# Attention and a squared-ReLU channel mix on one core: the left-over keys of two pairs multiplied in four quadrants, the token mix through PSUM

## The chip, the cores and the metric

The kernel runs on one core of a Trainium2 chip. The metric is the device time of one execution in microseconds (us). Engines: TensorE (PE; PEld are its weight loads), VectorE (DVE), ScalarE (ACT), GpSimd (POOL), and SyncE (SP), which here only issues transfers.

## The reference

Soft-capped attention over 8 batches, 12 heads, 448 tokens, 64 channels a head, then a channel mix in which each token is blended with the one before it:

```python
scores = cap * np.tanh(scale * q @ k.T / cap)
attn = np.exp(scores - max);  attn = attn / (attn.sum(-1) + 1e-9)
x = (attn @ v) as (B, S, 768)
xk = mu_k * x + (1 - mu_k) * x_prev          # x_prev: x one token earlier
xr = mu_r * x + (1 - mu_r) * x_prev
k = np.maximum(xk @ w_k, 0)                  # 768 -> 1024
out = sigmoid(xr @ w_r) * (k * k @ w_v)      # w_v: 1024 -> 768
```

All inputs are float32, `w_k`, `w_v`, `w_r` are float64.

## The kernel before

**Stages.** A first loop of 55 steps does the attention of 48 pairs of heads (six a batch), the rounding of the float64 weights, and, from step 7 on, the key product `xk @ w_k`. Its result and `x` go to DRAM. A second stage of 28 chunks of 128 tokens computes `xr @ w_r`, `k * k @ w_v` and the output; the change does not touch it.

**The order of a step.** Nothing is scheduled by a tool: each engine runs its instructions in the order in which the string `STEP` names the operations. Step i works on several pairs at once: scores (`S0` to `S3`), `tanh`, `exp`, `red` on pair i; `V` (values), `gather`, `recip`, `rec_store`, `rec_load` on pair i - 1; `norm`, `mix_old`, `mix_new`, `x_high`, `x_low`, `x_store` on pair i - 2; `qk_high`, `qk_low` on i + 2 and `load_qk` on i + 3. `K` (four in a step) is a quarter of the step's key product, 6 matmuls; `f` is one of the five VectorE operations that round a weight tile; up to step 9, five steps load a second weight tile.

**Scores.** A pair has two heads, h = 0 and 1. Queries and keys lie with head 0 on partitions 0 to 63 and head 1 on 64 to 127, so scores of both heads run as two matmuls of 64 rows each. The 448 keys are cut into three groups g of 128 and 64 left over. Each product is made of three (high by high, low by high, high by low). The left-over keys of both heads make one group, g = 3: head 0's 64 scores on the first half of the partitions, head 1's on the second. `tanh` and `exp` on ScalarE turn the scores (`s` in PSUM, two buffers) into `p`.

**Values.** `values` multiplies the exponentials by v, in float32: for each group two matmuls, one a head, each with 64 columns of the stationary tile `rv` and so half of the array's columns; `pv[p, 0:S]` gets head h on its half of the partitions. In group 3 the stationary tile of a head has v on that head's half of the rows, and zeros on the other, since the moving rows hold the exponentials of both heads:

```python
nc.tensor.matmul(pv[p, 0:S], v[:, g, h, :], ph[:, h if g < 3 else 0, :], start=(g == 0), stop=(g == 3))
```

`pv` has two buffers (`ps_v`), each a PSUM bank.

**Sums.** `red` on VectorE sums the exponentials over keys into `r1`, by a transposing reduction (one for each of g = 0 to 2, two halves for g = 3). A step later `gather` brings four parts of `r1` together by four transfers (`sq`), `recip` sums them, inverts and transposes (three VectorE instructions), `rec_store` writes the 2 x 448 results to DRAM (`rec_d`), and `rec_load` reads them back, spread over 64 partitions a head (`r`). One more step later `norm` writes `X = pv * r`.

**The mix.** `mix_old` (ScalarE) writes `xk = (1 - mu_k) * X` one token back, `mix_new` (VectorE) adds `mu_k * X` to it, `x_high` and `x_low` (GpSimd) split the sum into a high and a low half for the key product.

**The key product.** `kpart` issues the matmuls of `K`. A feature chunk of 128 takes 18 of them; its sum `kps` has two PSUM buffers, emptied by `relu` on ScalarE, which stands at three places of a step. The order in `key_order` delays the last of six pairs of a batch, so that two chunks end together in a batch's second step (step 6b + 2), and the next `K` then needs a buffer that the relu behind `exp2` frees.

**Queues.** All transfers but `k_store` are issued on SP, in the order of `STEP`; an issue that waits holds up those behind it. `load_qk` stands behind `rec_load`, which waits until `rec_store` has landed.

Of the kernel before, what the change touches and what calls it, by code (L numbers as in the profile page):

```python
# [9 lines left out]
F32 = mybir.dt.float32  # L10
F32R = mybir.dt.float32r
AF = mybir.ActivationFunctionType
ALU = mybir.AluOpType
# [3 lines left out]
B, H, S, D = 8, 12, 448, 64  # L17
# [8 lines left out]
P = 128  # L26
# [9 lines left out]
KM = 3 * P  # L36
KC = KM + P
LAG = 7
HALF = (slice(0, 64), slice(64, 128))
NB = 2 * S // 32  # L40
# [3 lines left out]

STEP = """gather load_v weight_load more weight_low S0 S1 V S2 f f f f f weight_rest tanh0 exp0 red0 norm
weight_sum tanh1 recip rec_store exp1 red1 mix_old mix_new K qk_high qk_low x_high x_low tanh2 relu k_store
K exp2 red2 relu k_store S3 K K tanh3 exp3 red3 relu k_store weight_abs rec_load load_qk x_store weight_store"""


def f(ap):
# [3 lines left out]
class Body:  # L56
# [61 lines left out]
    def init_sums(self, pool):  # L118


        nc = self.nc
        self.r1, self.sq, self.sr = [], [], []
        for j in range(2):
            self.r1.append(pool.tile([P, NB, 4], F32, name=f"r1_{j}"))
            nc.gpsimd.memset(self.r1[j], 0.0)
            for h in range(2):
                p = slice(64 - 64 * h, 96 - 64 * h)
                nc.vector.tensor_copy(self.r1[j][p, h * NB // 2:(h + 1) * NB // 2, 3], self.grd[p].to_broadcast([32, NB // 2]))
            self.sq.append(pool.tile([32, 4, NB, 4], F32, name=f"sq_{j}"))
            self.sr.append(pool.tile([32, 32], F32, name=f"sr_{j}"))  # L130
            nc.gpsimd.memset(self.sr[j], 1.0)

    def init_attn(self):
        self.raw, self.QK, self.rawv, self.S, self.P32, self.PV, self.R, self.rs = ({} for _ in range(8))

# [4 lines left out]
            self.nc.sync.dma_start(t[:, c], self.qk[i // NP, i % NP][:, c])  # L142

    def load_v(self, i):
        t = self.rawv[i] = self.rawp.tile([P, 4, 2, D], F32, name="rv")
        self.nc.sync.dma_start(t.rearrange("p c h d -> p (c h d)"), self.v[i // NP, i % NP])

    def qk_high(self, i, e="p"):
# [10 lines left out]
    def row_maxima(self, i):  # L159

        nc, qk = self.nc, self.QK[i]
        m = self.up.tile([S // 4, 8], F32, name="m", bufs=1)
        for h in range(2):
            t = HALF[h]
            for c in range(4):
                if c % 2 == 0:
                    s = self.ps_s.tile([P, 2, 512], F32, name="s")
                o = s[0:S // 4, c % 2, 0:S]
                for k, w in ((slice(0, KM), KM), (slice(KM, S), 64)):
                    first = S + (KM + 64 * h if w == 64 else 0)  # L170
                    for n, (a, b) in enumerate(((0, 0), (1, 0), (0, 1))):
                        nc.tensor.matmul(o[:, k], qk[b][t, c * S // 4:(c + 1) * S // 4], qk[a][t, first:first + w],
                                         start=(n == 0), stop=(n == 2))
                nc.vector.reduce_max(m[:, 4 * h + c:4 * h + c + 1], o, axis=mybir.AxisListType.X)
        nc.scalar.activation(m, m, AF.Tanh, scale=self.scl_t[0:S // 4])
        nc.vector.tensor_scalar(m, m, self.cap_t[0:S // 4], None, op0=ALU.mult)
        nc.sync.dma_start(self.max_d.rearrange("h (c p) -> p (h c)", c=4), m)
        self.M = self.up.tile([P, 2, S], F32, name="M", bufs=1)
        for h in range(2):
            nc.sync.dma_start(self.M[:, h], self.max_d[h:h + 1, :].to_broadcast([P, S]))  # L180
# [12 lines left out]

    def tanh(self, i, g):
        n = 2 if g < 3 else 1
        p32 = self.p32p.tile([P, n, S], F32, name=f"p32_{n}", bufs=5 if g < 3 else 2)
        self.nc.scalar.activation(p32, self.S.pop((i, g))[:, :n, 0:S], AF.Tanh, scale=self.scl_t)  # L197
        self.P32[i, g] = p32

    def exp(self, i, g):  # L200
        p32 = self.P32[i, g]
        if self.maxima:
            for h in range(2):
                p, c = (slice(0, P), h) if g < 3 else (HALF[h], 0)
                self.nc.vector.scalar_tensor_tensor(out=p32[p, c, :], in0=p32[p, c, :], scalar=self.cap_t[p],
                                                    in1=self.M[p, h, :], op0=ALU.mult, op1=ALU.subtract)
        self.nc.scalar.activation(p32, p32, AF.Exp, scale=1.0 if self.maxima else self.cap_t)  # L207

    def values(self, i):

        nc, v = self.nc, self.rawv.pop(i)
        pv = self.ps_v.tile([P, 512], F32, name="pv")
        for g in range(4):
            ph = self.P32.pop((i, g))
            for h, p in enumerate(HALF):
                nc.tensor.matmul(pv[p, 0:S], v[:, g, h, :], ph[:, h if g < 3 else 0, :], start=(g == 0), stop=(g == 3))  # L216
        self.PV[i] = pv

    def red(self, i, g):
        r1, p32 = self.r1[i % 2], self.P32[i, g]
        for p, h, out in [(slice(0, P), slice(0, 2), r1[:, :, g])] if g < 3 else \
                [(HALF[h], slice(0, 1), r1[HALF[h], h * NB // 2:(h + 1) * NB // 2, 3]) for h in range(2)]:
            self.nc.vector.tensor_reduce(out=out, in_=p32[p, h].rearrange("p h (b k) -> p (h b) k", k=32),  # L225
                                         axis=mybir.AxisListType.X, op=ALU.add, apply_transpose=True)

# [19 lines left out]
        self.R[i] = r  # L247

    def norm(self, i):
        self.nc.vector.tensor_mul(self.X[i % 2][:, 1:], self.PV.pop(i)[:, 0:S], self.R.pop(i))  # L250

    def mix_old(self, i):
        b, hp = i // NP, i % NP
        if hp == 0:
            xh = self.xkp[b % 2].tile([P, ND, S], F32R, name="xkh", tag="xkh")
            xl = self.xkp[b % 2].tile([P, ND, S], F32R, name="xkl", tag="xkl")
            self.XK[b] = (xh, xl)
        self.xk = self.up.tile([P, S], F32, name="xk", bufs=1)
        self.nc.scalar.mul(self.xk, self.X[i % 2][:, 0:S], self.om["k"][:, hp:hp + 1])

    def mix_new(self, i):
        hp = i % NP
        self.nc.vector.scalar_tensor_tensor(out=self.xk, in0=self.X[i % 2][:, 1:], scalar=self.mu["k"][:, hp:hp + 1],  # L263
                                            in1=self.xk, op0=ALU.mult, op1=ALU.add)

    def x_high(self, i, e="p"):
        self.copy(e, self.XK[i // NP][0][:, i % NP, :], self.xk)
# [193 lines left out]
    def step(self, i, KS):  # L461
# [6 lines left out]
        pair.update(dict.fromkeys("norm mix_old mix_new x_high x_low x_store".split(), i - 2))  # L468
        for op in STEP.split():
            j = pair.get(op)  # L470
# [142 lines left out]
def _layout(inputs):  # L613
    c = np.ascontiguousarray
    qk = np.zeros((B, NP, 2, D, S + KC), np.float32)
    v = np.zeros((B, NP, 2, 64, 4, 2, D), np.float32)
    vp = inputs["v"].reshape(B, NP, 2, S, D)
    qk[..., :S] = inputs["q"].reshape(B, NP, 2, S, D).swapaxes(3, 4)
    kt = inputs["k"].reshape(B, NP, 2, S, D).swapaxes(3, 4)
    qk[..., S:S + KM] = kt[..., :KM]  # L620
    v[..., :3, :, :] = vp[:, :, :, :KM].reshape(B, NP, 2, 3, 2, 64, D).transpose(0, 1, 4, 5, 3, 2, 6)
    for h in range(2):
        qk[:, :, h, :, S + KM + 64 * h:S + KM + 64 * h + 64] = kt[:, :, h, :, KM:]
        v[:, :, h, :, 3, h] = vp[:, :, h, KM:]
    mu = lambda a: c(a.reshape(ND, P).T)
    return {
        "qk": qk.reshape(B, NP, P, S + KC),
        "v": v.reshape(B, NP, P, 8 * D),
        "cap": np.asarray(inputs["cap"]).reshape(1, 1),
        "muk": mu(inputs["moe_mu_k"]),  # L630
        "mur": mu(inputs["moe_mu_r"]),
        "wk": c(inputs["moe_w_k"]).view(np.int64),
        "wv": c(inputs["moe_w_v"]).view(np.int64),
        "wr": c(inputs["moe_w_r"]).view(np.int64),
    }
# [15 lines left out]
```

## Time and profile before

| | |
|---|---|
| three runs | 1011.4, 1012.74, 1013.64 us; median 1012.74 |
| the profiled execution | 1016.09 us; its span from first to last instruction 1014.3 us |
| granted TensorE clock, mean | 0.976 of full speed |
| busy, share of the span | PE 95%, PEld 77%, DVE 66%, ACT 49%, POOL 29% |
| V (`L216`) | 768 records, 163.6 us |
| scores (`L189`) | 1008 records, 232.5 us |
| key product (`L298`) | 1152 records, 431.7 us |
| second stage (`L441`) | 2352 records, 602.4 us |
| DVE reductions (`L225`) | 240, 215.0 us |
| DVE mix (`L263`) | 48, 42.6 us |
| ACT tanh, exp (`L197`, `L207`) | 192 each, 173.1 and 182.5 us |

Busy is the time in which an engine has at least one instruction running; a group's busy time is that of its own instructions, so groups whose matmuls overlap add up to more than the span. Counts of TensorE are those of the hardware's records: a float32 product in the code leaves two, the split ones (float32r) one each. In a timeline row stand start, length, engine, line, operation, output and inputs, shapes, count, and in square brackets how long the engine was idle before it and what ended that. `64*128` is the part of the array that a matmul uses, rows by columns.

### The profile page before, as it was taken

The page shows a single profiled execution, that of the slowest core. Times are in us where ns is not written, and L with a number is a line of the kernel's source. Part 1 is how long each engine was busy: PE and PEld are TensorE (multiplying, and loading weights), DVE is VectorE, ACT ScalarE, POOL GpSimd, SP SyncE. Part 2 cuts the span into 40 slices and gives each one's busy share as a digit, 9 for nine tenths or more (in the row PEclk, how much of TensorE's full clock was granted, in tenths as well). Part 3 has the DMA queues.
Part 4 walks back from the last instruction along what each step waited for, and adds up shares of the span by engine and source line. Part 5 has one row for each costly group of instructions (what it writes and reads, how often), then busy time and mean ns, then how long its engine had stood idle before and what let it go on. Part 6 is the DMA issues. An engine that isn't in the chain of part 4 may idle for free.

```text
span 1014.3 us, 14549 instructions
## 1 busy us (share of the span) xinstructions
PE 967.1 (95%) x5280; PEld 781.6 (77%) x5280; DVE 667.6 (66%) x1202; ACT 500.3 (49%) x626; POOL 297.6 (29%) x267
## 2 busy tenths in 40 slices
PE   6678899999999999999999999999999999999997
PEld 3234566666666766766667899999999999999997
DVE  6999998777777777777556477455445544554550
ACT  6766678777788877777777212221122112211220
POOL 4555555554546454555442230000000000000000
PEclk8778999999999999999999999999999999999999
DMA  4555556666665666665552665233233323332320
GB/s 153 143 150 148 172 150 175 211 199 182 179 217 186 194 173 195 194 193 157 151 152 92 224 191 137 81 105 104 70 87 105 103 68 90 104 100 64 98 68 35
DMA packets 121249, 142.01 MB, mean 140 GB/s; under 512 B 19280, under 2 KB 100048, under 8 KB 121168
## 3 DMA queue, kind: packets, MB, share of 16 engines
q1 hardware_dynamic: 111952, 126.30, 43.5%
q10 hardware_dynamic: 9216, 14.68, 3.9%
q8 instruction: 44, 0.72, 0.3%
q14 instruction: 37, 0.30, 0.1%
HBM read 95.79 MB, written 42.40 MB: 136 GB/s over the span
## 4 chain that ended last, share of the span: by engine, by line
PE 61%; DVE 16%; DMA 14%; ACT 4%; issue 2%; SPq 1%; POOL 1%; ACTq 0%; DVEq 0%; POOLq 0%
PE pvv L441 22%; PE pr L441 17%; PE kps L298 10%; PE pv L216 7%; DMA sq<-r 6%; PE s L189 6%; DVE r L225 5%; DMA r<-rec_d 4%; ACT p L197 1%; DVE xk L263 1%; DMA rec_d<-rs 1%; DVE sr L234 1%; ACT p L207 1%; DVE wa L361 1%; SPq L230 1%
## 5 line engine op out<-in xcount | busy, mean ns | idle before, releaser
L225 DVE TRANSPOSE_TENSOR_REDUCE r<-p 128x28 f32<-128x896 f32 (+1 forms) x240 | 215.0, 905 | 44.5 <-ACT p L207 41.8
L197 ACT ACTIVATE p<-s,scl_t 128x896 f32<-128x896 f32 x192 | 173.1, 901 | 40.5 <-PE s L189 36.2
L207 ACT ACTIVATE p<-p,cap_t 128x896 f32<-128x896 f32 x192 | 182.5, 951 | 11.1 <-ACT ko L305 5.3
L74 ACT CAST xh<-t 128x768 fp32r<-128x768 f32 x27 | 22.7, 839 | 307.5 <-DVE t L424 307.5
L216 PE MATMUL pv<-p,rv 128*64 128x448 f32 x768 | 163.6, 570 | 0.0
L298 PE MATMUL kps<-xkh,wkh 128*128 128x448 f32 x384 | 147.4, 384 | 10.2 <-ACT ko L305 10.1
L456 DVE TENSOR_TENSOR o<-pvv,rsg 128x768 f32<-128x768 f32 (+1 forms) x29 | 27.0, 930 | 181.6 <-PE pvv L441 180.7
L298 PE MATMUL kps<-xkl,wkh 128*128 128x448 f32 x384 | 142.2, 370 | 0.0
L298 PE MATMUL kps<-xkh,wkl 128*128 128x448 f32 x384 | 142.1, 370 | 0.0
L216 PEld LDWEIGHTS pv<-p,rv 128*64 128x64 f32 x768 | 53.2, 143 | 89.5 <-issue 82.0
L441 PE MATMUL pvv<-wvh,kl 128*128 128x384 f32 x448 | 115.2, 335 | 0.0
L441 PE MATMUL pvv<-wvh,kh 128*128 128x384 f32 x448 | 115.2, 335 | 0.0
L441 PE MATMUL pvv<-wvl,kh 128*128 128x384 f32 x448 | 115.2, 335 | 0.0
L189 PE MATMUL s<-qkh 64*128 64x448 f32 (+1 forms) x336 | 85.6, 451 | 30.0 <-ACT p L197 25.0
L80 POOL TENSOR_TENSOR qkl<-rqk,qkh 128x960 fp32r<-128x960 f32 x47 | 105.9, 2253 | 3.9
L189 PEld LDWEIGHTS s<-qkh 64*128 64x128 f32 (+1 forms) x336 | 37.4, 191 | 87.4 <-ACT p L197 35.8
L298 PEld LDWEIGHTS kps<-xkh,wkh 128*128 128x128 f32 x384 | 73.2, 191 | 31.0 <-issue 13.1
L441 PE MATMUL pr<-wrh,xl 128*128 128x384 f32 x336 | 85.6, 336 | 0.8 <-DVE xl L432 0.8
L441 PE MATMUL pr<-wrh,xh 128*128 128x384 f32 x336 | 85.7, 336 | 0.1
L441 PE MATMUL pr<-wrl,xh 128*128 128x384 f32 x336 | 85.5, 335 | 0.0
L372 POOL TENSOR_TENSOR wsq<-wa,wsq 128x384 f32<-128x384 f32 x44 | 44.4, 1010 | 138.1 <-DVE wsq L365 138.1
L441 PEld LDWEIGHTS pvv<-wvl,kh 128*128 128x128 f32 x448 | 81.0, 188 | 0.0
(66 smaller groups left out, 1467.8 us busy)
## 6 DMA issues: line engine op xcount, KB each, us to landing
rqk<-qk SPq DMA_DIRECT2D x47, 480.0 KB
k_d<-ko ACTq DMA_DIRECT2D x64, 224.0 KB
kr<-k_d SPq DMA_DIRECT2D x28, 512.0 KB
rv<-v SPq DMA_DIRECT2D x48, 256.0 KB
x_d<-x SPq DMA_DIRECT2D x48, 224.5 KB
r<-rec_d SPq DMA_DIRECT2D x96, 112.0 KB
out<-o SPq DMA_DIRECT2D x27, 384.0 KB
xc<-x_d SPq DMA_DIRECT2D x24, 387.0 KB
```

The costliest lines, as they stand in the source:

```text
L74: self.nc.scalar.copy(out, x)
L80: {"p": self.nc.gpsimd, "v": self.nc.vector}[e].tensor_sub(*a)
L189: nc.tensor.matmul(s[:, h, 0:S], qk[a][p, k], qk[b][p, 0:S], start=(n == 0), stop=(n == 2))
L197: self.nc.scalar.activation(p32, self.S.pop((i, g))[:, :n, 0:S], AF.Tanh, scale=self.scl_t)
L207: self.nc.scalar.activation(p32, p32, AF.Exp, scale=1.0 if self.maxima else self.cap_t)
L216: nc.tensor.matmul(pv[p, 0:S], v[:, g, h, :], ph[:, h if g < 3 else 0, :], start=(g == 0), stop=(g == 3))
L225: self.nc.vector.tensor_reduce(out=out, in_=p32[p, h].rearrange("p h (b k) -> p (h b) k", k=32), axis=mybir.AxisListType.X, op=ALU.add, ap ...
L230: self.nc.sync.dma_start(self.sq[i % 2][:, q], self.r1[i % 2][32 * q:32 * q + 32])
L298: nc.tensor.matmul(self.kps[fc][:, 0:S], w, m[:, dc, :], start=first, stop=last)
L372: {"p": self.nc.gpsimd, "v": self.nc.vector}[e].tensor_add(sq, f(a), sq)
L441: self.nc.tensor.matmul(ps[:, m, 0:HN], a[:, c, :], w[:, c, m * HN:m * HN + HN], start=(c == 0 and part == 0), stop=(c == n - 1 and part = ...
L456: nc.vector.tensor_mul(o[:, q], pv[:, q, 0:HN], rs[:, q])
```

## The change

It does five things.

1. **Quadrants.** In odd pairs the left-over keys of the two heads change places (head 0 on the second half of the partitions), in the data's layout, in `exp` (with maxima), `red` and the guards of the sums. `values` leaves group 3 out and keeps it in `self.tails`. With the odd pair of each two, four products of 64 rows by 64 columns follow, without zeros: even pair, head 0: rows 0 to 63, columns 0 to 63; head 1: rows and columns 64 to 127; odd pair, head 0: rows 64 to 127, columns 0 to 63; head 1: rows 0 to 63, columns 64 to 127. The two pairs' sums lie in different PSUM banks.
2. **Buffers.** `rv` has three instead of two, the left-over exponentials three instead of two.
3. **Mix.** `mix_old` writes into the pair's `pv` bank rather than into SBUF, `mix_new` reads it there and writes `xk`. The bank is free after `mix_new`, where it was after `norm`.
4. **Order.** `norm` goes behind `red1` (it stood behind `red0`), with `recip` and `rec_store` behind it; `mix_old` and `mix_new` go behind `tanh2`.
5. **SP queue.** `load_qk` goes ahead of `rec_load`.

The diff without the layout and the sums:

```diff
-STEP = """gather load_v weight_load more weight_low S0 S1 V S2 f f f f f weight_rest tanh0 exp0 red0 norm
-weight_sum tanh1 recip rec_store exp1 red1 mix_old mix_new K qk_high qk_low x_high x_low tanh2 relu k_store
-K exp2 red2 relu k_store S3 K K tanh3 exp3 red3 relu k_store weight_abs rec_load load_qk x_store weight_store"""
+STEP = """gather load_v weight_load more weight_low S0 S1 V S2 f f f f f weight_rest tanh0 exp0 red0
+weight_sum tanh1 exp1 red1 norm recip rec_store K qk_high qk_low tanh2 mix_old mix_new x_high x_low relu k_store
+K exp2 red2 relu k_store S3 K K tanh3 exp3 red3 relu k_store weight_abs load_qk rec_load x_store weight_store"""
...
-        t = self.rawv[i] = self.rawp.tile([P, 4, 2, D], F32, name="rv")
+        t = self.rawv[i] = self.rawp.tile([P, 4, 2, D], F32, name="rv", bufs=3)
...
-        p32 = self.p32p.tile([P, n, S], F32, name=f"p32_{n}", bufs=5 if g < 3 else 2)
+        p32 = self.p32p.tile([P, n, S], F32, name=f"p32_{n}", bufs=5 if g < 3 else 3)
...
-        pv = self.ps_v.tile([P, 512], F32, name="pv")
-        for g in range(4):
+        self.PV[i] = pv = self.ps_v.tile([P, 512], F32, name="pv")
+        for g in range(3):
             ph = self.P32.pop((i, g))
             for h, p in enumerate(HALF):
-                nc.tensor.matmul(pv[p, 0:S], v[:, g, h, :], ph[:, h if g < 3 else 0, :], start=(g == 0), stop=(g == 3))
-        self.PV[i] = pv
+                nc.tensor.matmul(pv[p, 0:S], v[:, g, h, :], ph[:, h, :], start=(g == 0), stop=False)
+        self.tails.append((i, v))
+        if i % 2:
+            for j, v in self.tails:
+                ph = self.P32.pop((j, 3))
+                for h, p in enumerate(HALF):
+                    t = HALF[(h + j) % 2]
+                    nc.tensor.matmul(self.PV[j][p, 0:S], v[t, 3, h, :], ph[t, 0, :], start=False, stop=True)
+            self.tails = []
...
-        self.xk = self.up.tile([P, S], F32, name="xk", bufs=1)
-        self.nc.scalar.mul(self.xk, self.X[i % 2][:, 0:S], self.om["k"][:, hp:hp + 1])
+        self.xold = self.PV.pop(i)[:, 0:S]
+        self.nc.scalar.mul(self.xold, self.X[i % 2][:, 0:S], self.om["k"][:, hp:hp + 1])
...
+        self.xk = self.up.tile([P, S], F32, name="xk", bufs=1)
         self.nc.vector.scalar_tensor_tensor(out=self.xk, in0=self.X[i % 2][:, 1:], scalar=self.mu["k"][:, hp:hp + 1],
-                                            in1=self.xk, op0=ALU.mult, op1=ALU.add)
+                                            in1=self.xold, op0=ALU.mult, op1=ALU.add)
```

Three places show what the engines now get. Lines of the changed kernel stand some ten further down. First TensorE around V, in a step in the middle of the loop, before (`p_2_...` are exponentials of groups 0 to 2, `p_1_...` those of the left-over keys; numbers tell buffers apart):

```order
L216 MATMUL pv<-p_2_3103,rv 64x448 x2
L216 MATMUL pv<-p_2_3109,rv 64x448 x2
L216 MATMUL pv<-p_2_3134,rv 64x448 x2
L216 MATMUL pv<-p_1_3161,rv 64x448 x2
L189 MATMUL s<-qkh 128x448 x2
```

and in the changed kernel, in the step whose V is of an odd pair:

```order
L190 MATMUL s<-qkl,qkh 128x448 x2
L217 MATMUL pv<-p_2_3101,rv 64x448 x2
L217 MATMUL pv<-p_2_3106,rv 64x448 x2
L217 MATMUL pv<-p_2_3127,rv 64x448 x2
L225 MATMUL pv<-p_1_3041,rv 64x448 x2
L225 MATMUL pv<-p_1_3159,rv 64x448 x2
L190 MATMUL s<-qkh 128x448 x2
```

The left-over products of two pairs stand behind each other here, in the step before there are none.

VectorE in the middle of one step, before (`r_0` are the sums, `sq` the gathered ones, `x` the normalised pair):

```order
L225 TENSOR_REDUCE r_0_188<-p_2_2981 128x28
L250 TENSOR_TENSOR x_156<-pv,r 128x448
L234 TENSOR_REDUCE sr_200<-sq_199 32x28
L236 RECIPROCAL sr_200<-sr_200 32x28
L238 STREAM_TRANSPOSE rs<-sr_200 32x32
L225 TENSOR_REDUCE r_0_188<-p_2_2987 128x28
L263 SCALAR_TENSOR_TENSOR xk<-x_156,mu_k,xk 128x448
L225 TENSOR_REDUCE r_0_188<-p_2_3011 128x28
```

and after:

```order
L234 TENSOR_REDUCE r_0_188<-p_2_2981 128x28
L234 TENSOR_REDUCE r_0_188<-p_2_2986 128x28
L259 TENSOR_TENSOR x_156<-pv,r 128x448
L243 TENSOR_REDUCE sr_200<-sq_199 32x28
L245 RECIPROCAL sr_200<-sr_200 32x28
L247 STREAM_TRANSPOSE rs<-sr_200 32x32
L274 SCALAR_TENSOR_TENSOR xk<-x_156,mu_k,pv 128x448
L234 TENSOR_REDUCE r_0_188<-p_2_3006 128x28
```

The second reduction has moved ahead of the normalising and of the gathered sums, and the mix reads `pv`.

ScalarE in one of the steps 6b + 2, from the second tanh on, before:

```order
L197 ACTIVATE p_2_3226<-s,scl_t 128x896
L207 ACTIVATE p_2_3226<-p_2_3226,cap_t 128x896
L259 ACTIVATE xk<-x_156,om_k 128x448
L197 ACTIVATE p_2_3252<-s,scl_t 128x896
L207 ACTIVATE p_2_3252<-p_2_3252,cap_t 128x896
L305 ACTIVATE ko<-kps 128x448 x2
L311 DMA k_d<-ko 128x448 x2
```

and after:

```order
L198 ACTIVATE p_2_3225<-s,scl_t 128x896
L208 ACTIVATE p_2_3225<-p_2_3225,cap_t 128x896
L198 ACTIVATE p_2_3245<-s,scl_t 128x896
L269 ACTIVATE pv<-x_156,om_k 128x448
L208 ACTIVATE p_2_3245<-p_2_3245,cap_t 128x896
L316 ACTIVATE ko<-kps 128x448 x2
L322 DMA k_d<-ko 128x448 x2
```

The mix has moved behind the third tanh; the third exponential and the two relus, which free the banks of the key product, stand behind it as before.

More of the change, by code (lines that the diff above doesn't have):

```diff
@@ L126, in init_sums @@
             for h in range(2):
-                p = slice(64 - 64 * h, 96 - 64 * h)
+                p = slice(64 - 64 * ((h + j) % 2), 96 - 64 * ((h + j) % 2))
                 nc.vector.tensor_copy(self.r1[j][p, h * NB // 2:(h + 1) * NB // 2, 3], self.grd[p].to_broadcast([32, NB // 2]))
@@ L169, in row_maxima @@
                 for k, w in ((slice(0, KM), KM), (slice(KM, S), 64)):
-                    first = S + (KM + 64 * h if w == 64 else 0)
+                    first = S + (KM + 64 * ((h + i) % 2) if w == 64 else 0)
                     for n, (a, b) in enumerate(((0, 0), (1, 0), (0, 1))):
@@ L203, in exp @@
             for h in range(2):
-                p, c = (slice(0, P), h) if g < 3 else (HALF[h], 0)
+                p, c = (slice(0, P), h) if g < 3 else (HALF[(h + i) % 2], 0)
                 self.nc.vector.scalar_tensor_tensor(out=p32[p, c, :], in0=p32[p, c, :], scalar=self.cap_t[p],
@@ L211, in values @@
         nc, v = self.nc, self.rawv.pop(i)
-        pv = self.ps_v.tile([P, 512], F32, name="pv")
-        for g in range(4):
+        self.PV[i] = pv = self.ps_v.tile([P, 512], F32, name="pv")
+        for g in range(3):
             ph = self.P32.pop((i, g))
             for h, p in enumerate(HALF):
-                nc.tensor.matmul(pv[p, 0:S], v[:, g, h, :], ph[:, h if g < 3 else 0, :], start=(g == 0), stop=(g == 3))
-        self.PV[i] = pv
+                nc.tensor.matmul(pv[p, 0:S], v[:, g, h, :], ph[:, h, :], start=(g == 0), stop=False)
[6 more added lines that the diff above has]
+                    nc.tensor.matmul(self.PV[j][p, 0:S], v[t, 3, h, :], ph[t, 0, :], start=False, stop=True)
+            self.tails = []
     def red(self, i, g):
@@ L223, in red @@
         for p, h, out in [(slice(0, P), slice(0, 2), r1[:, :, g])] if g < 3 else \
-                [(HALF[h], slice(0, 1), r1[HALF[h], h * NB // 2:(h + 1) * NB // 2, 3]) for h in range(2)]:
+                [(HALF[(h + i) % 2], slice(0, 1), r1[HALF[(h + i) % 2], h * NB // 2:(h + 1) * NB // 2, 3]) for h in range(2)]:
             self.nc.vector.tensor_reduce(out=out, in_=p32[p, h].rearrange("p h (b k) -> p (h b) k", k=32),
@@ L249, in norm @@
     def norm(self, i):
-        self.nc.vector.tensor_mul(self.X[i % 2][:, 1:], self.PV.pop(i)[:, 0:S], self.R.pop(i))
+        self.nc.vector.tensor_mul(self.X[i % 2][:, 1:], self.PV[i][:, 0:S], self.R.pop(i))
     def mix_old(self, i):
@@ L622, in _layout @@
     for h in range(2):
-        qk[:, :, h, :, S + KM + 64 * h:S + KM + 64 * h + 64] = kt[:, :, h, :, KM:]
-        v[:, :, h, :, 3, h] = vp[:, :, h, KM:]
+        for odd in range(2):
+            t = (h + odd) % 2
+            qk[:, odd::2, h, :, S + KM + 64 * t:S + KM + 64 * t + 64] = kt[:, odd::2, h, :, KM:]
+            v[:, odd::2, t, :, 3, h] = vp[:, odd::2, h, KM:]
     mu = lambda a: c(a.reshape(ND, P).T)
```

## The prediction

> **What bounds the kernel now.** I read the page first, for where each engine is full, then the windows view with a cut at each place where the fullest engine changes. Times are us from the span's start.
>
> ```profile
> PE 967.1 (95%) x5280; PEld 781.6 (77%) x5280; DVE 667.6 (66%) x1202; ACT 500.3 (49%) x626; POOL 297.6 (29%) x267
> PE   6678899999999999999999999999999999999997
> DVE  6999998777777777777556477455445544554550
> ...
> 22.81:116.40 93.59, 68.83 (x308) 36.45 (x309) 88.95 (x140) 62.30 (x80) 51.20 (x51) 0.82 0.49 145
> 116.40:549.77 433.37, 425.49 (x2320) 289.93 (x2319) 323.60 (x546) 336.16 (x424) 219.76 (x186) 0.99 0.61 179
> 549.77:610.00 60.23, 59.57 (x306) 50.60 (x306) 35.94 (x55) 15.21 (x22) 15.20 (x15) 1.00 0.60 192
> 610.00:1014.30 404.30, 398.35 (x2293) 397.40 (x2292) 203.09 (x434) 72.35 (x83) 0.00 (x0) 1.00 0.32 88
> ```
>
> The window columns after the length are PE, PEld, DVE, ACT, POOL busy with counts, the granted clock, DMA share, GB/s. From 23 to 116 us (steps 2 to 8 of the attention loop) VectorE is full, 88.95 of 93.59. From 116 to 550 (38 steps, 9 to 46) TensorE is, 425.49 of 433.37. The last 404 us are the second stage, which the change does not touch. So the change can pay in two places: VectorE's work in seven steps, and TensorE's work, or its waits, in 38. The timeline of one undisturbed step shows what TensorE does with its time:
>
> ```profile
> 299.78 0.47 PE L189 MATMUL s<-qkh 64*128 64x448 f32 x2
> ...
> 300.90 0.37 PE L189 MATMUL s<-qkl,qkh 64*128 64x448 f32 x2
> 301.20 3.23 PE L216 MATMUL pv<-p,rv 128*64 128x448 f32 x16
> ...
> 304.36 0.47 PE L189 MATMUL s<-qkh 64*128 64x448 f32 x2
> 304.67 0.37 PE L189 MATMUL s<-qkh,qkl 64*128 64x448 f32 x2
> 304.87 0.36 PE L189 MATMUL s<-qkl,qkh 64*128 64x448 f32 x2
> ...
> 310.84 0.47 PE L189 MATMUL s<-qkh 64*128 64x448 f32 x2
> ```
>
> One step is 310.84 - 299.78 = 11.06 us, with V, the value products, from 301.20 to 304.36. Scores run as two row halves at once, a couple each 0.20 (304.67 to 304.87). For V I asked two instants, its beginning and its end:
>
> ```profile
> 301.20 0.60 PE L216 MATMUL pv<-p,rv 128*64 128x448 f32 x2
> 303.88 0.55 PE L216 MATMUL pv<-p,rv 128*64 128x448 f32 x2
> ```
>
> There are two matmuls in flight at either end. Sixteen records in couples are eight slots, and from the first to the last start (301.20 to 303.88) are seven, so a slot is 2.68 / 7 = 0.38 us. Each product of the code is two records, so group g of keys takes two slots, the left-over group too, although half of each of its stationary tiles is zeros.
>
> **The tails.** For every couple of pairs (even, odd) the change removes two tails, 4 slots, and adds four products of 64 rows by 64 columns in four different quadrants. If all four run at once, they take 2 slots. The couple saves 2 x 0.38 = 0.77. It adds one more change of the array's shape, 128*64 to 64*64. A change from 64*128 to 128*64 stands above: 300.90 to 301.20 is 0.30 where 0.20 is the rhythm, 0.10 lost, and the first slot after it can lose as much again; I take 0.2. Net 0.57 a couple. Steps 9 to 48 have 20 couples: **-11.4 us**. Bounds: -15 (no price for the shape) and, if quadrants do not overlap as I think, the rivals below. Couples before step 9 lie under VectorE and are costed at nothing. The price appears in odd pairs' steps, which become 11.26 long, and even pairs' steps become 10.29.
>
> **Mix through PSUM.** The sum of old and new tokens is the same VectorE instruction on 448 columns; one of its two inputs moves from SBUF to PSUM.
>
> ```profile
> 22.80:150.00 127.20, 17.21 (x10) 0.87 0.52 152
> 150.00:580.00 430.00, 25.43 (x39) 0.99 0.60 179
> ...
> 22.80:150.00 127.20, 5.87 (x10) 0.87 0.52 152
> ...
> 71.22 2.24 POOL L80 TENSOR_TENSOR qkl<-rqk,qkh 128x960 fp32r<-128x960 f32 x1
> ...
> 72.06 1.88 DVE L263 SCALAR_TENSOR_TENSOR xk<-x,mu_k,xk 128x448 f32<-128x448 f32 x1
> ```
>
> The first two rows are L263 alone (the mix), the third L250 alone (the normalising, which reads PSUM and SBUF). The early ten mixes take 1.72 on average, the later ones 0.65; the normalising takes 0.59 in the same early stretch. The last two rows show why: the mix at 72.06 stands over GpSimd's two-input subtraction and ends 0.48 after it (73.46 to 73.94), as if it had waited. With PSUM as one input it looks like the normalising, so I take 0.65: 1.23 saved in each of the seven VectorE-bound steps, -8.6. The next work on VectorE, the last reductions, then waits some 0.25 a step for the exponentials behind ScalarE's moved mix: **-7 us**. Bounds: 0 (it still waits for GpSimd) and -9. The Trainium skill, "SBUF — State Buffer", section "Who interferes with whom", says that a VectorE instruction with two SBUF inputs is blocked by a GpSimd instruction that reads SBUF, and one with at most a single SBUF input is not; both kinds of rows above agree with it, the moved form has no row yet, and by that rule the whole 8.6 would come.
>
> **The order.** The normalising goes behind the second reduction and ahead of the reciprocal, ScalarE's mix behind the third tanh, and load_qk ahead of rec_load on the SP queue. What this meets is in the waits and in two steps, the one from 310.84 and the worst one, 38:
>
> ```profile
> DVE sr L234 <- DMA sq<-r: 62.7, 30, 4.1
> ACT xk L259 <- DVE x L250: 61.7, 29, 5.3
> PEld kps L298 <- ACT ko L305: 12.7, 7, 4.1
> ...
> 308.31 0.37 PE L298 MATMUL kps<-xkh,wkh 128*128 128x448 f32 x1
> ...
> 311.75 1.01 ACT L197 ACTIVATE p<-s,scl_t 128x896 f32<-128x896 f32 x1 [1.46 <-PE s L189]
> 312.34 0.36 DVE L357 TENSOR_SCALAR wt<-wsq 128x384 f32<-128x384 f32 x1
> 314.60 1.11 DVE L225 TRANSPOSE_TENSOR_REDUCE r<-p 128x28 f32<-128x896 f32 x1
> 314.77 1.04 ACT L207 ACTIVATE p<-p,cap_t 128x896 f32<-128x896 f32 x1
> 315.63 0.59 DVE L250 TENSOR_TENSOR x<-pv,r 128x448 f32<-128x448 f32 x1
> 316.31 0.67 ACT L259 ACTIVATE xk<-x,om_k 128x448 f32<-128x448 f32 x1 [0.50 <-DVE x L250]
> 318.06 0.61 DVE L234 TENSOR_REDUCE sr<-sq 32x28 f32<-32x448 f32 x1 [1.84 <-DMA sq<-r]
> ...
> 445.12 0.61 DVE L234 TENSOR_REDUCE sr<-sq 32x28 f32<-32x448 f32 x1 [3.53 <-DMA sq<-r]
> ...
> 453.41 0.59 DVE L250 TENSOR_TENSOR x<-pv,r 128x448 f32<-128x448 f32 x1
> 454.09 0.67 ACT L259 ACTIVATE xk<-x,om_k 128x448 f32<-128x448 f32 x1 [3.10 <-DVE x L250]
> 456.63 0.96 ACT L305 ACTIVATE ko<-kps 128x448 f32<-128x448 f32 x2
> 457.21 0.74 PE L298 MATMUL kps<-xkh,wkh 128*128 128x448 f32 x1 [2.91 <-ACT ko L305]
> ```
>
> In seven steps (6b + 2, where two key sums end together) TensorE waits 12.7 in all for relu to free its bank. Step 38 shows the chain: the gathered sums land late (445.12), VectorE falls behind, the normalising comes at 453.41, ScalarE stands 3.10 at its mix, relu is late, TensorE stands 2.91. After the change the second reduction and the normalising, 1.11 + 0.59 = 1.7, are done before VectorE stands at the gather, so a late gather puts the next step back by 1.7 less; load_qk no longer stands behind rec_load, which waits for a store to land, so the gather stands less far behind its transfer. The rec_load behind it comes later by one issue, and is needed a step later. Against that, the normalising stands behind one more reduction. A normal step, counted from its start at 310.84: exponential 1 ends at 315.81, 4.97; second reduction 5.0 to 6.1; normalising to 6.7 (before: 5.4); ScalarE does the third tanh meanwhile, to 6.0 or 6.6, stands at most 0.8, mixes to 7.4, exponential 2 to 8.5, relu to 9.0. TensorE asks for the bank 308.31 - 299.78 = 8.5 into a step, 8.7 with the longer V, so each of the seven waits 0.3 or more. The longest, 4.1, keeps 3, since all the weight work still stands ahead of it; step 38's 3.3 loses 1.7; I give the five others 0.6: 3 + 1.6 + 3 = 7.6 for 12.7: **-5 us**. Bounds: -12.7 and +7 (one more microsecond in each).
>
> ScalarE's half of the mix now writes PSUM, which no row has. The same 448 columns take 0.67 from SBUF (316.31) and 0.48 from PSUM (relu, 456.63), so I allow 0.2 either way, under ScalarE's slack of 97 us in the 433. The third buffers of rv and of the left-over exponentials cost nothing: same transfers, same counts. The pv bank is held until VectorE's mix, some 9.3 into its step; its next user is V of the following step, 1.4 into that, so 3 us of cover, and without it V would begin later by what is lacking.
>
> Does the longer chain become the bound? The ring from one normalising to the next: 0.59, mix 0.67, exponential 1.04, relu with its store 0.9 (an estimate: twice the 0.48), and, from these rows,
>
> ```profile
> 308.51 0.64 ACT L197 ACTIVATE p<-s,scl_t 128x448 f32<-128x448 f32 x1 [0.42 <-PE s L189]
> ...
> 309.18 0.67 ACT L207 ACTIVATE p<-p,cap_t 128x448 f32<-128x448 f32 x1
> ...
> 310.02 2.29 DVE L225 TRANSPOSE_TENSOR_REDUCE r<-p 128x28 f32<-128x896 f32 x3
> ```
>
> tanh 3 0.64, exponential 3 0.67, the two half reductions 2.29 - 1.11 = 1.18, five weight operations 2.26 (312.34 to 314.60), two reductions 2.2: 10.15, and some 0.5 for eight hand-overs: 10.65. TensorE's mean step becomes (11.26 + 10.29) / 2 = 10.78. It stays the bound by 0.13, so the ring costs nothing in the forecast.
>
> **Sum.** -11.4 - 7 - 5 = -23.4. The profiled execution took 1016.09 (span 1014.3), which gives 992.7; the median of the runs is 3.35 below it, so I forecast 989.
>
> **Rivals.** First, the ring: if the hand-overs take 0.85 rather than 0.5, it is 11.0 and holds the step there, and of the 11.4 only 38 x 0.06 = 2.3 is left: 1012.7 - 2.3 - 7 - 2 = 1001 (the relu waits, which hang on the same chain, then give 2 rather than 5). For it speaks that ScalarE's 61.7 us of waits are just this chain; against it, that they hold TensorE in seven steps only.
>
> Second, the four products run in a staircase: each is two records, and if the second of one must start before the first of the next may, the four take 5 slots, the couple 17 where it took 16: 0.38 + 0.2 = +0.58, x 20 = +11.6, less the other terms' 12: 1012, no change. The two matmuls in flight at the very first instant of V speak against it: a staircase begins with one. The Trainium skill, "TensorE: Matmul & The Clock Gate", section "Part 3: Packing small matmuls — row/col tiling", states that matmuls start and end strictly in program order; by that rule the staircase and its 1012 would come, and the trace of V so far does not agree with it.
>
> Third, slower: products that share a column half but stand in different row halves, or share rows and differ in columns, exclude each other here, and the four run one by one: 8 slots, the couple 20 for 16, 4 x 0.38 + 0.2 = +1.7, x 20 = +34, less 12: 1035. It turns the gain to a loss from about 5 slots on, where the four cost what the other terms bring (12 / 20 = 0.6 a couple). Scores overlap rows and V overlaps columns, both in the rows above, which speaks against it; both at once has no row.
>
> **How the numbers follow.** Forecast 0.66, within 981 to 1000 by the bounds of its small terms; ring 0.14 at 1001; staircase 0.10 at 1012; one by one 0.06 at 1035; 0.04 for one in which the relu waits vanish too (-7.6 more: 981 and below). From 978 to 1010 all but about 0.16 is held. A change under 0.2% (2 us) cannot be told from none. Faster: forecast, ring, the fast rest and a fifth of the staircase, 0.86; within 0.2%: 0.05; slower: 0.09.
>
> **What would show it.** In V of even pairs, 12 records and some 2.4 us; in V of odd pairs four tail matmuls in flight at once, 3.3 us in all: steps of 10.3 and 11.3 in turn. The mix at 0.63 also before 150 us, and VectorE's stretch from step 2 to 8 about 7 shorter. Waits of TensorE for relu near 8 in all, 12.7 now. Wrong would be: tail matmuls starting two by two; ScalarE standing before its mix and TensorE before scores in every step; the mix still at 1.9.

## The result, and the profile after

The changed kernel takes 989.25 us (median of four runs, 987.76 to 990.2), where the kernel before took 1012.07 beside it (1010.97 to 1013.64): ratio 0.977, 95% interval 0.975 to 0.979. The profiled execution took 987.76, its span 985.8. From its page, the engines' shares, TensorE's row over the span and the chain of work that ended last:

```profile
PE 945.5 (96%) x5280; PEld 766.8 (78%) x5280; DVE 660.8 (67%) x1202; ACT 498.9 (51%) x626; POOL 296.4 (30%) x267
PE   6668999999999999999999999999999999999997
...
PE 80%; DVE 9%; ACT 4%; DMA 3%; issue 1%; SPq 1%; POOL 0%; DVEq 0%; ACTq 0%; POOLq 0%
```

The chain has 3% of transfers in it; on the page of before it had 14%. The windows view of after, cut where the same steps begin as in the cut of before (step 9 and step 47), columns as there:

```profile
20.26:105.95 85.69, 61.15 (x311) 31.80 (x311) 80.70 (x141) 62.37 (x80) 53.82 (x52) 0.84 0.53 163
105.95:519.90 413.95, 413.32 (x2321) 280.53 (x2320) 326.30 (x548) 334.89 (x425) 219.33 (x186) 1.00 0.59 187
519.90:582.00 62.10, 60.61 (x314) 51.28 (x314) 36.41 (x56) 14.96 (x22) 14.48 (x15) 1.00 0.62 196
582.00:985.80 403.80, 397.09 (x2286) 396.14 (x2284) 202.74 (x433) 72.42 (x83) 0.00 (x0) 1.00 0.31 87
```

Step 9 begins at 105.95 where it began at 116.40: 10.45 gained. Steps 9 to 46 take 413.95 where they took 433.37: 19.4 gained. From step 47 on, 1.4 is given back. In the loop (steps 9 to 46) TensorE now stands for 0.6 of 414 us; before it was 7.9 of 433. The timeline of TensorE in two steps of after that follow each other, around V:

```profile
280.87 0.47 PE L190 MATMUL s<-qkh 64*128 64x448 f32 x2
...
282.30 2.48 PE L217 MATMUL pv<-p,rv 128*64 128x448 f32 x12
...
284.70 0.47 PE L190 MATMUL s<-qkh 64*128 64x448 f32 x2
...
291.28 0.47 PE L190 MATMUL s<-qkh 64*128 64x448 f32 x2
...
292.70 2.48 PE L217 MATMUL pv<-p,rv 128*64 128x448 f32 x12
295.11 0.98 PE L225 MATMUL pv<-p,rv 64*64 64x448 f32 x8
296.02 0.47 PE L190 MATMUL s<-qkh 64*128 64x448 f32 x2
...
302.66 0.47 PE L190 MATMUL s<-qkh 64*128 64x448 f32 x2
```

The first step is 10.41 long, its V 2.40 (282.30 to 284.70; before 3.16). The second is 11.38, one of those with a short relu wait; without one they take 11.31. Its tail is 0.91 (295.11 to 296.02). The same timeline, asked for what is in flight at two instants of the tail:

```profile
295.11 0.61 PE L225 MATMUL pv<-p,rv 64*64 64x448 f32 x4
...
295.54 0.56 PE L225 MATMUL pv<-p,rv 64*64 64x448 f32 x4
```

Four records at a time: four quadrants at once, two slots. The groups of lines give the mix (mean of one after the bar's comma, in ns) over all 48 steps:

```profile
L274 DVE SCALAR_TENSOR_TENSOR xk<-x,mu_k,pv 128x448 f32<-128x448 f32 x48 | 30.5, 636 | 1.0 <-ACT pv L269 0.8 <-ACT ko L316 0.2
```

None is long any more. The last view is of waits, over the whole execution (us in all, count, longest):

```profile
PEld kps L309 <- ACT ko L316: 4.6, 8, 2.8
...
DVE sr L243 <- DMA sq<-r: 1.1, 1, 1.1
```

TensorE's waits for relu fell from 12.7 to 4.6, VectorE's waits for the gathered sums from 62.7 to 1.1. The second is the larger surprise, and the experiments turn on it. A first theory was the forecast's: three terms that add up, quadrants, mix, and a normalising that is done before VectorE stands at the gather. Its rivals: that the quadrants' slots pay only where other waits allow it; and that the gather itself came earlier, by the place of load_qk.

### The profile page after: what moved, and what is told of

It reads as the page before. It is cut to its first block, busy times and chain, and to the rows that moved or that the text cites. A ratio compares the mean times of both kernels' runs of the same rounds, so it can differ in the third digit from the quotient of the medians.

```text
span 985.8 us, 14561 instructions
## 1 busy us (share of the span) xinstructions
PE 945.5 (96%) x5280; PEld 766.8 (78%) x5280; DVE 660.8 (67%) x1202; ACT 498.9 (51%) x626; POOL 296.4 (30%) x267
## 4 chain that ended last, share of the span: by engine, by line
PE 80%; DVE 9%; ACT 4%; DMA 3%; issue 1%; SPq 1%; POOL 0%; DVEq 0%; ACTq 0%; POOLq 0%
PE pvv L452 23%; PE kps L309 19%; PE pr L452 17%; PE s L190 11%; PE pv L217 9%; DVE r L234 3%; ACT p L208 2%; PE pv L225 2%; DMA wst<-w_d 1%; ACT p L198 1%; DVE wt L368 1%; DVE wa L372 1%; DVE wkl L396 1%; DVE wa L370 1%; DMA sq<-r 1%
## 5 line engine op out<-in xcount | busy, mean ns | idle before, releaser
L234 DVE TRANSPOSE_TENSOR_REDUCE r<-p 128x28 f32<-128x896 f32 (+1 forms) x240 | 220.2, 922 | 81.0 <-ACT p L208 76.6
L217 PE MATMUL pv<-p,rv 128*64 128x448 f32 x576 | 124.1, 568 | 0.0
L190 PE MATMUL s<-qkh 64*128 64x448 f32 (+1 forms) x336 | 84.7, 445 | 29.2 <-ACT p L198 24.2
L383 POOL TENSOR_TENSOR wsq<-wa,wsq 128x384 f32<-128x384 f32 x44 | 44.4, 1009 | 159.8 <-DVE wsq L376 146.2
L217 PEld LDWEIGHTS pv<-p,rv 128*64 128x64 f32 x576 | 38.4, 142 | 64.2 <-issue 54.1
## 6 DMA issues: line engine op xcount, KB each, us to landing
x_d<-x SPq DMA_DIRECT2D x48, 224.5 KB
```

What stands on the lines that cost most here:

```text
L190: nc.tensor.matmul(s[:, h, 0:S], qk[a][p, k], qk[b][p, 0:S], start=(n == 0), stop=(n == 2))
L217: nc.tensor.matmul(pv[p, 0:S], v[:, g, h, :], ph[:, h, :], start=(g == 0), stop=False)
L383: {"p": self.nc.gpsimd, "v": self.nc.vector}[e].tensor_add(sq, f(a), sq)
```

## Experiments

In all of them the kernel before ran beside them at 1016.7 to 1016.9 (1009 to 1023 in single runs), so they are compared by ratio or with the whole change on the same footing, which is the last of the second group: 988.66.

**The parts alone.** First the quadrants alone, with their layout and buffers, `STEP` and the mix as before:

```diff
-STEP = (order of the change)
+STEP = (order of before)
...
-        self.xold = self.PV.pop(i)[:, 0:S]
+        self.xk = self.up.tile([P, S], F32, name="xk", bufs=1)
...
```

> Only the quadrants (with their layout and third buffers); order and mix as before. A couple of pairs was seen to save two slots, 0.75, and to pay 0.17 for the shape and 0.18 for a slower rhythm of the key product: -0.40, so by the theory that TensorE's saved slots are a term of their own, 20 couples give -8: 1004. By the rival theory, that the step was held by the waits between the engines and the slots only pay once these are gone: 1011 to 1013.

1013.97, ratio 0.998 (0.996 to 1.001): no gain that can be told from none, the rival's answer. Steps of 10.41 and 11.31 are there. Its windows view for steps 9 to 46:

```profile
114.67:546.30 431.63, 416.00 (x2320) 281.55 (x2319) 323.35 (x546) 334.50 (x424) 219.64 (x186) 1.00 0.62 180
```

Its waits in the same stretch, of TensorE's weight loads and of its matmuls for relu:

```profile
PEld kps L307 <- ACT ko L314: 12.8, 6, 3.6
PE kps L307 <- ACT ko L314: 10.7, 5, 3.2
```

TensorE is busy 9.5 less (416.0 for 425.5), and the loop is 1.7 shorter (431.63 for 433.37). In the same stretch of before the two rows read 8.2 and 6.5. TensorE's matmuls wait 4.2 more for relu, and 3.4 more (4.8 for 1.4) for ScalarE's tanh, which frees the score buffers: the slots were saved and handed to waits.

Then the order alone, on the kernel before:

```diff
-STEP = (order of before)
+STEP = (order of the change)
```

> Only the order (normalising behind the second reduction, mix behind the third tanh, load_qk ahead of rec_load). By the forecast's terms -5 (relu waits alone): 1007. By the rival, that the order also gave the early stretch its gain, because VectorE no longer stands at the gather there, and most of the relu waits: -5 to -10 more, 997 to 1002.

1009.0, ratio 0.993 (0.990 to 0.996). Both expectations missed in part: 7.9 less than before beside it, between the 5 of the one and the 10 or more of the other. In the profile the loop fell to 424.1 (before 433.4), with the relu wait in it down from 8.2 to 2.9 and nearly every step at 11.06, but the early stretch gained nothing: step 9 begins at 116.33.

The mix alone:

```diff
...
+        self.xold = self.PV.pop(i)[:, 0:S]
+        self.nc.scalar.mul(self.xold, self.X[i % 2][:, 0:S], self.om["k"][:, hp:hp + 1])
...
```

> Only the mix through PSUM. By the forecast's term VectorE's mix falls from 1.9 to 0.63 in seven steps that VectorE bounds: -7, 1005. By the rival, that the early stretch is held by the ring of VectorE and ScalarE and not by VectorE's sum of work: 1010 to 1012, with the mix at 0.63 all the same.

1010.83, ratio 0.995 (0.993 to 0.997). No mix takes over 0.7 in its profile, and the early stretch is the one that changed, by its windows view:

```profile
22.80:110.20 87.40, 65.12 (x301) 35.00 (x301) 81.47 (x140) 61.30 (x79) 51.12 (x51) 0.82 0.53 154
```

Step 9 begins at 110.20, 6.2 earlier, and VectorE's busy time there is 81.47 where it was 88.95. This term came close to its forecast (7).

**Do four quadrants run at once?** The whole change, but odd pairs keep the halves of even ones, so that a couple's four products use two quadrants:

```diff
-                    t = HALF[(h + j) % 2]
+                    t = HALF[h]
...
```

(The left-out lines make the same replacement in the data's layout, `exp`, `red` and the guards.)

> The whole change, but odd pairs keep the halves of even ones: the four left-over products of a couple use two quadrants, twice each. If four quadrants at once are what saves the slots, the tail takes 4 slots, 0.75 more for each of 20 couples: +15, 1004. If products of 64 rows overlap in any case, or the tail is hidden, 989 to 991.

1003.09, ratio 0.987 (0.984 to 0.991). Its timeline, the tail and the scores behind it:

```profile
279.26 1.72 PE L225 MATMUL pv<-p,rv 64*64 64x448 f32 x8
280.91 0.47 PE L190 MATMUL s<-qkh 64*128 64x448 f32 x2
```

And what is in flight at the tail's first instant:

```profile
279.26 0.59 PE L225 MATMUL pv<-p,rv 64*64 64x448 f32 x2
```

Two at a time, and 1.65 from the tail's start to the next scores where the four quadrants took 0.91: two slots more. Long steps are 12.00 instead of 11.31. The quadrants are the mechanism, and without a wait in the way the slots show nearly in full: 19 x 0.69 = 13 of the 14.4 between 1003.09 and 988.66.

**Two parts of three, and the queue.** Quadrants and mix with the old order; quadrants and order with the old mix; the whole change with load_qk behind rec_load; and the whole change again:

```diff
-K exp2 red2 relu k_store S3 K K tanh3 exp3 red3 relu k_store weight_abs load_qk rec_load x_store weight_store"""
+K exp2 red2 relu k_store S3 K K tanh3 exp3 red3 relu k_store weight_abs rec_load load_qk x_store weight_store"""
```

> Quadrants and mix through PSUM, the order as before. If the order is what takes the relu waits away, they stay as long as with the quadrants alone (15 to 18 us in all) and the short steps of 10.4 pay little: 1003 to 1007 on a chip where before takes 1013 to 1017. If the mix alone already frees VectorE enough: 990 to 996.

> Quadrants and order, the mix in SBUF. The loop from step 9 on should be as after the whole change (414 us, relu waits under 6), and only the early stretch longer, by the ten mixes of 1.9: 6 to 10 more than the whole change. If PSUM also matters in the loop: more than 10.

> The whole change, but load_qk behind rec_load again. If the relu waits went because VectorE no longer stands at a late gather, the place of load_qk matters little: within 2 of the whole change. If the gather came late because of load_qk's transfer just ahead of it: waits of 5 to 8 come back.

> The whole change once more, beside the others on this chip, as their measure: 0.977 of before, short and long steps of 10.4 and 11.3, relu waits of 5.

Quadrants and mix: 1006.05, ratio 0.990 (0.986 to 0.993). VectorE waits 84.7 for the gather, TensorE 12.2 for relu (15 to 18 expected): without the order the loop stays at 431.0. Quadrants and order: 999.01, ratio 0.982 (0.978 to 0.986), 10.4 more than the whole, at the edge of what was expected. Its loop (415.9) is within 2.4 of the whole change's, and the early stretch is 8.6 longer: PSUM matters there. Old queue: 999.48, ratio 0.983 (0.979 to 0.987), with the normalising in its new place. The waits of that kernel, whole execution:

```profile
DVE sr L243 <- DMA sq<-r: 75.1, 35, 3.4
...
PEld kps L309 <- ACT ko L316: 12.1, 8, 2.7
```

So the new places of normalising and mix do not take the waits away. With the old queue they are worth something all the same: 999.48 against 1006.05 for quadrants and mix, the executions apart (998.2 to 1002.9 against 1003.6 to 1007.5), and 5.5 in steps 9 to 46 (from 108.53 to 534.05, 425.5, where it was 431.0).

What is left of the order is the swap of two transfers on the SP queue, tried alone below. The timeline shows how it works. In the kernel with the old queue, one step, two of the SP queue's issues and VectorE's use of the gathered sums:

```profile
299.77 0.54 SPq L143 DMA_DIRECT2D rqk<-qk  x1
...
301.35 2.46 SPq L239 DMA_DIRECT2D sq<-r  x4
...
306.92 0.61 DVE L243 TENSOR_REDUCE sr<-sq 32x28 f32<-32x448 f32 x1 [2.05 <-DMA sq<-r]
```

The same two issues in the whole change (its second profile):

```profile
290.24 0.34 SPq L143 DMA_DIRECT2D rqk<-qk  x1
...
293.42 2.45 SPq L239 DMA_DIRECT2D sq<-r  x4
```

With the old order load_qk's 480 KB are issued 1.6 before the gather's 56 KB (4 of 14), with the new one 3.2 before. VectorE takes the sums up 5.6 after the gather's issue there, waiting 2.05 for them; with the new order it does not wait. Between the two stand `x_store` (224.5 KB) and `weight_store` (192 KB), in both kernels.

The trace also keeps the packets of the transfers, which their sizes tell apart (3840 bytes in load_qk, 448 in the gather). With the old queue load_qk's packets run from 300.99 to 304.56, and the gather's from 304.35 to 305.83: the first starts 3.00 after the gather's first issue. With the new one load_qk's are through at 293.22, before the gather is issued, and the gather's run from 295.13 to 296.73: the first starts 1.71 after the issue. Over steps 9 to 46 the gather's last packet ends 4.37 after its first issue with the old queue and 3.44 after it in the whole change (medians). The Trainium skill, "DMA: Bandwidth & Descriptors", section "Two DMAs through the same engine are not ordered", says that within one queue of one transfer engine descriptors start in order and overlap; these packets, which begin in the order of issue and overlap, agree with it.

One microsecond counts here because the gather closes a ring: from its issue to VectorE's use of the sums, 5.57 in this step; to the issue of `rec_store`, 1.22; through the queue's issues to the next gather, 4.91; 11.70 in all. VectorE waits for the gather in 34 of the loop's 38 steps with the old queue, and a step takes 11.20 on average (425.52 / 38), where TensorE's own length is (10.41 + 11.31) / 2 = 10.86. The swap shortens the ring: the gather lands sooner, and load_qk's issue falls into the time in which `rec_load` waits for the store to land (0.43 behind `rec_store`, 290.24 for 289.81, where it stood 2.51 behind it, 299.77 for 297.26).

**The queue alone.** The kernel before with that swap only, and the whole change with normalising and mix in their old places:

```diff
-K exp2 red2 relu k_store S3 K K tanh3 exp3 red3 relu k_store weight_abs rec_load load_qk x_store weight_store"""
+K exp2 red2 relu k_store S3 K K tanh3 exp3 red3 relu k_store weight_abs load_qk rec_load x_store weight_store"""
```

> The kernel before with one edit: load_qk ahead of rec_load on the SP queue. If that alone brings the gather in time, VectorE's wait for it falls from 63 us to under 5, and the relu waits with it, though the normalising stays behind the first reduction: 9 to 10 less in the loop, as with the whole new order, 1004 to 1009. If the place of the normalising is what cures it: 1013 to 1017, as before.

> The whole change with normalising and mix back in their old places; only load_qk stays ahead. If the queue did it, within 3 of the whole change (986 to 992). If the new places carry a part of their own: 993 to 1000.

The swap alone: 1005.05, ratio 0.989 (0.986 to 0.993), a larger gain than that of quadrants or mix alone, and no smaller one than that of the whole order alone (0.993). Its windows view for steps 9 to 46:

```profile
116.07:538.29 422.22, 421.20 (x2320) 288.86 (x2320) 338.29 (x544) 338.01 (x424) 219.20 (x186) 1.00 0.58 182
```

Its waits for the gathered sums, whole execution:

```profile
DVE sr L234 <- DMA sq<-r: 4.5, 4, 2.5
```

422.2 is 38 x 11.06 and 1.9 more; TensorE stands for 1.0. The whole change with the old places: 990.55, ratio 0.975 (0.972 to 0.978) against 0.973 (0.970 to 0.977) for the whole change. With the swap, where the normalising stands makes no difference that these runs can tell. Beside quadrants and mix in the old places the swap is worth 15.5 (1006.05 to 990.55).

**Two variants of the whole change.** In one, the low halves of the key weights are subtracted on GpSimd, since VectorE still bounds the early stretch. In the other, the four products are issued head by head:

```diff
-            self.nc.vector.tensor_sub(lo, sq, f(hi))
+            self.nc.gpsimd.tensor_sub(lo, sq, f(hi))
```

```diff
-            for j, v in self.tails:
-                for h, p in enumerate(HALF):
+            for h, p in enumerate(HALF):
+                for j, v in self.tails:
...
```

> The whole change, with the 16 low halves of the key weights (0.56 each on VectorE, all in steps 2 to 8) subtracted on GpSimd. If VectorE's chain bounds the early stretch now, it falls by 5 to 9: 980 to 984. If GpSimd's lock on VectorE's second input or a late low half eats it: 987 to 992.

> The whole change, with the four left-over products issued head by head rather than pair by pair, so that two that share a column half stand behind each other. If four queues run side by side, the order does not matter: 988 to 990, four starts within 0.03. If neighbours that share columns or rows hold each other up, the tail takes 3 or 4 slots: 995 to 1004. If the slower rhythm of the key product hangs on what the tail leaves behind, it can go: 985.

GpSimd: 991.82, ratio 0.976 (0.973 to 0.980), no gain: the first expectation missed, and the time lies in the range of the second (987 to 992). The early window of the whole change (its second profile):

```profile
20.00:106.00 86.00, 61.75 (x311) 31.40 (x310) 80.59 (x140) 62.20 (x80) 53.68 (x52) 0.84 0.53 162
```

The same window of the variant:

```profile
20.00:106.00 86.00, 61.06 (x304) 30.54 (x302) 81.31 (x130) 61.15 (x78) 62.06 (x60) 0.84 0.52 158
```

VectorE's first weight operation in the groups of lines, whole execution, of the change:

```profile
L368 DVE TENSOR_SCALAR wt<-wsq 128x384 f32<-128x384 f32 x44 | 19.4, 441 | 7.3 <-ACT wsq L348 6.2
```

And of the variant:

```profile
L368 DVE TENSOR_SCALAR wt<-wsq 128x384 f32<-128x384 f32 x44 | 22.7, 515 | 8.3 <-ACT wsq L348 7.2
```

VectorE runs ten instructions fewer in the window and is as busy, since others last longer while GpSimd is busy 8.4 us more: this one 515 ns where it took 441. In the window alone, this operation and the one behind it (`L370`) take 9.4 + 8.8 = 18.2 us in eleven each, where they took 7.2 + 4.8 = 12.0; the ten subtractions had taken 5.1. Head by head: 989.3, ratio 0.973 (0.970 to 0.977); the tail is again eight records in 0.98, so the order of the four does not matter. No variant beats the whole change.

## Why the prediction was right, point by point

The forecast of 989 met 989.25, but not by the sum it stood on. Against the profiled executions the sum was -23.4, and they differ by 28.3 (1016.09 to 987.76). The offset of 3.35 to the median, which I took over from before, does not hold for after, whose profiled execution is its fastest: its median is 1.5 above it. Why, is not shown: beside the experiments before scattered from 1009 to 1023 and the whole change from 988.3 to 990.0, but in the four executions of each that give the result both spread alike (2.7 and 2.4). The tails brought less than forecast, the order more, and the offset was wrong by as much as was left: that the total met to 0.3 is luck. The places where the change pays, and that four quadrants run at once, were forecast rightly.

- **The tails, -11.4.** Measured 19 x 0.40 = 7.6 in steps 9 to 46 (10.41 + 11.31 against 2 x 11.06). Two slots saved (0.75) and the price of the shape (0.17: tail and changes in the long step, 0.2 forecast) stood. What was mis-sized is the rest of the step, which I took as fixed: the key product's matmuls run 0.207 apart where they ran 0.202, 24 of them in a step, 0.09 in every step (below).
- **Where the tails pay.** The forecast counted them in full because TensorE was busy in the loop. Alone they paid 1.7 of it. They needed the waits gone. Couples before step 9, costed at nothing, paid some: step 9 begins 1.7 earlier with quadrants alone, 3.5 with quadrants beside the mix (106.73 for 110.20).
- **Mix through PSUM, -7.** 6.2 alone; 8.6 as the difference in the early stretch between the change with and without it (115.3 to 106.8). The mechanism is shown in the mix's own rows: 10 of 1.56 to 1.93 before, none over 0.7 after (0.626 to 0.682). In the swap-only kernel 28 of the 48 mixes last over 1 us (ten before), at no cost in the loop, where VectorE has room. ScalarE's half into PSUM took 0.64 (0.67 before). That the bank of `pv` is held longer cost nothing in the whole change, as forecast; in the loop of quadrants and mix with the old order V waited 4.2 for the mix.
- **The order, -5.** The failing step. Its size in the loop was 11.8 (433.37 less 413.95, less the tails' 7.6), and its reason was wrong in the main: I gave most of it to the 1.7 of work that is done ahead of the gather, and called load_qk's place a help. The swap alone took VectorE's wait from 62.7 to 4.5; the new places without the swap left 75.1; with the swap and without the new places nothing measurable was missing. The new places are a second, weaker cure: 6.6 with the old queue (1006.05 to 999.48), nothing on top of the swap. I took the gather's lateness as given and did not lay out the ring that makes it.
- **What a wait costs.** The forecast priced TensorE's waits at their length, but the loop gave 11.8 where TensorE had stood for 7.9 in all. At least part of the rest is matmuls that ran slower behind two of the three long waits (steps 20 and 38): with the swap alone TensorE is busy 421.2 on as many records (2320) as took 425.5. In the timeline of before, step 38, just behind the wait that ends at 457.21:

```profile
457.75 0.57 PE L298 MATMUL kps<-xkh,wkl 128*128 128x448 f32 x1
458.12 0.57 PE L298 MATMUL kps<-xkl,wkh 128*128 128x448 f32 x1
458.50 0.57 PE L298 MATMUL kps<-xkh,wkh 128*128 128x448 f32 x1
```

The key product's matmuls run 0.37 apart here, up to 460.36, where 0.20 is the rhythm. By the windows view the granted clock is 0.50 from 457.2 to 459.0; it is 1.00 from 450 to 454 and again from 461 to 463. The wait is 2.91, but the time from this step's V to the next one's is 15.66 instead of 11.06, 4.6 more. The prediction shows the first row behind the wait (0.74 long instead of 0.37) and does not price it.

Two points are left.

- **The ring.** The forecast left TensorE 0.13 of margin over the ring. In the loop it held: steps are TensorE's own length, and its standing adds up to 0.6. In the early stretch VectorE is busy 80.7 of 85.7 and still carries it. The forecast had no row for the other ring, through the SP queue and the gather; that one had no room left, and the swap gave it some.
- **The staircase** did not come: four starts together, then four. **One by one** did not come either.

What the 1.4 given back from step 47 on is, was not tried. The traces place 0.3 of it ahead of the second stage's first product and 1.0 behind.

## What to carry to other kernels

A wait that shows as "A waits for B's result" can have its cause in what was issued just ahead on the same transfer queue: before moving work on the engines, find the large transfer that stands before the small one that they wait for, and try to move that. Slots saved on a full engine are only worth what the next wait leaves of them; run each part alone and together, since here the quadrants shortened the loop by 1.7 alone, and by some 8.5 where the waits were gone (422.2 with the queue's swap to 413.5 to 413.9 with everything). A wait of the fullest engine can cost more than its length: read how fast it runs behind the wait. When a kernel's executions scatter, forecast from the profiled one to a profiled one, and do not take the offset to the median over from before.

## What the hardware showed that I had not expected

The key product's matmuls have two rhythms. In the timeline of before, two of them with ten intervals between, the second and the twelfth of a row:

```profile
305.47 0.36 PE L298 MATMUL kps<-xkh,wkl 128*128 128x448 f32 x1
...
307.49 0.37 PE L298 MATMUL kps<-xkl,wkh 128*128 128x448 f32 x1
```

The same two in a step of after:

```profile
285.82 0.37 PE L309 MATMUL kps<-xkh,wkl 128*128 128x448 f32 x1
...
287.89 0.36 PE L309 MATMUL kps<-xkl,wkh 128*128 128x448 f32 x1
```

Ten intervals take 2.02 before and 2.07 after, at the same granted clock and with the same instructions. Steps of 10.29 instead of 10.41 in the same execution (step 33) run at the faster one again, and steps with the quadrants alone had the slower one too. It costs some 3.5 us over the loop; what sets it was not found, and the order of the four products was not it.
